# New priorities and engine choices for the first two batches and the weights of an attention and maxout kernel

## The chip, the cores and the metric

The kernel runs on one core of a Trainium2 chip. The time is device time in microseconds (us) of one execution of the whole program, and its figure is the median of several runs. The core's engines are TensorE (PE, matrix products), VectorE (DVE), ScalarE (ACT), GpSimd (POOL) and SyncE (SP, which here only issues DMAs). Each engine works through its own queue of instructions in a fixed order and waits where an instruction's inputs or buffers are not ready.

## The reference

Two attentions are added, and the sum goes through a maxout layer with an output projection. All is fp32.

```python
# q, k, v: 8 batches, 8 heads, 576 positions, head dim 64
factor = 4
scale = 1.0 / np.sqrt(D)
q_d = q.reshape(B, H, Sd, factor, D).mean(axis=3)      # and k_d, v_d
out_d = sm_attn(q_d, k_d, v_d)                         # 144 x 144 softmax attention
out_up = np.repeat(out_d, factor, axis=2)
mask = np.abs(pos[:, None] - pos[None, :]) < factor    # a band of 7 positions
scores = np.where(mask, scale * np.matmul(q, k.transpose(0, 1, 3, 2)), -1000000000.0)
out_local = np.matmul(softmax(scores), v)              # written out in the original
x = (out_up + out_local).transpose(0, 2, 1, 3).reshape(B * S, H * D)   # 4608 x 512
h = np.maximum(np.maximum(x @ w1, x @ w2), x @ w3)     # 512 -> 768
return h @ w_out                                       # 768 -> 512
```

## The kernel before

**Precision.** A first- or second-layer product is made of three fp32r matmuls. Each operand is split into a high part (a cast, `xhi`, `whi`, `hh`, `wo`) and a low part (what the cast lost, `xlo`, `wlo`), and hi x hi, lo x hi and hi x lo are added up in PSUM.

**Blocks.** The work is done by batch: 8 blocks of 512 tokens, and a ninth that holds the 64 positions left over from all batches. A block's input has four tiles of 128 channels, each with an `xhi` and an `xlo`. `mlp_in` makes the first layer: 6 column blocks, each with 3 accumulations of 12 matmuls (216 in all). `mlp_out` makes the second layer: 72 matmuls over 6 pieces of `w_out`. The matmuls of both go to PSUM tag `pm` (3 banks); attention's go mostly to `pa` (5 banks).

**Attention.** A head group `n` is four heads of a batch (`n` 0 and 1 are batch 0, 2 and 3 batch 1). Batches 0 and 1 are made by `dense`, step by step: `q` and `v` load, `qk` pools q and k (tiles `hp`, `qkT`), `s0` and `s1` make the banded scores of two heads each and their softmax (`mx`, `sm`, `z`), `tail` and `vd` pool v (`traw`, `vtail`, `hv`, `vd`), `sums` makes the pooled scores and their softmax (`nz`, `pd`, `rd`, `ptld`, and after a transpose `pt`, `ptt`), `pv` the pooled values (`od`), and `v0` and `v1` the banded values. `v0` and `v1` copy transposed weights out of PSUM (`y`), add `od` to the product, which gives a finished tile (`t` for batch 0, `x` for batch 1), and split it into `xhi` and `xlo`. The later batches take another way, with products on ACT and POOL, and are not touched by the change.

**Weights.** w1, w2 and w3 come as 64-bit words, in 6 blocks (`rawin`, 3072 words of 32 bits in each of 128 partitions), and w_out in 6 pieces (in `pvb`). `weight_split` (printed below) makes fp32 of them: an absolute value on ACT, a clamp, an `and`, two `or`s on DVE, the cast to the high part and the subtraction for the low part.

**What sets the order.** No engine order is written by hand. The functions record operations, each with a priority: the number that `at(...)` sets for the step, alone or per engine. `Recorder.place` then simulates the engines with a price for each operation: of the operations at an engine's head it takes the one that can start first, and of those that can start at the same time the one with the lowest priority number. An operation with several forms goes to the engine that would end it first. The order that comes out is emitted (line 495 issues every instruction, so that line stands in all rows) and is then fixed. So a priority says what goes first where two operations are ready together, and since every choice shifts what is ready next, a few numbers can reorder a whole stretch.

**The numbers.** `PLAN[0]` and `PLAN[1]` hold the steps of batches 0 and 1 with a priority for each; `WLOAD` has the priority of the six weight blocks' loads and `WMAKE` that of their splits, `WOUT` that of all that is done for w_out, `BEGIN` that of the first steps of head group 4. MLP work has -100, and the split of a finished tile -200. `HOMES` fixes copies and casts to ACT ("A"), to DVE ("D") or leaves them to the planner ("-"): `norm` (the normalising of `sm`, one letter for each pair of heads), `band` (the copies `y`), `hi` (the weight casts, six blocks and then six pieces), `xhi`, `od`, `pt` and `late` (the copies of `pt`'s last part and of `ptt`).

The core of the choice, from `place`:

```python
key = (t if t > now + PATIENCE[e] else now, o.prio, o.seq)
if pick is None or key < pick[0]:
    pick = (key, o, t)
```

Of the kernel before, what the change touches and what calls it, by code (L numbers as in the profile page):

```python
# [38 lines left out]
PLAN = (
    (  # L40
        ("q", 0, -2480.0),
        ("v", 0, 905.0),
        ("qk", 0, -2340.0),
        ("s0", 0, {"PE": 1990.0, "DVE": 540.0, "ACT": 1780.0}),
        ("s1", 0, {"PE": -1905.0, "DVE": 65.0, "ACT": 1135.0}),
        ("tail", 0, {"DVE": -405.0, "SP": 480.0}),
        ("q", 1, -975.0),
        ("v", 1, 1150.0),
        ("sums", 0, {"PE": -1675.0, "DVE": -1840.0, "ACT": 260.0}),
        ("vd", 0, {"DVE": -1715.0, "SP": 740.0}),  # L50
        ("qk", 1, -130.0),
        ("s0", 1, {"PE": 15.0, "DVE": -1045.0, "ACT": 1125.0}),
        ("s1", 1, {"PE": 1165.0, "DVE": 235.0, "ACT": 315.0}),
        ("tail", 1, {"DVE": 3360.0, "SP": 2255.0}),
        ("pv", 0, {"PE": -430.0, "ACT": 3475.0}),
        ("v0", 0, {"PE": 195.0, "DVE": -280.0, "ACT": 80.0}),
        ("v1", 0, {"PE": 1795.0, "DVE": 10.0, "ACT": -795.0}),
        ("sums", 1, {"PE": 1905.0, "DVE": 95.0, "ACT": -60.0}),
        ("vd", 1, 3095.0),
        ("pv", 1, {"PE": 95.0, "ACT": 6225.0}),  # L60
        ("v0", 1, {"PE": 1800.0, "DVE": -1230.0, "ACT": 3665.0}),
        ("v1", 1, {"PE": 1685.0, "DVE": 2800.0, "ACT": 1870.0}),
    ),
    (
        ("q", 0, 165.0),
        ("v", 0, -2485.0),
        ("qk", 0, 910.0),
        ("s0", 0, {"PE": 1930.0, "DVE": 60.0, "ACT": 230.0}),
        ("s1", 0, {"PE": 1090.0, "DVE": 1560.0, "ACT": 1425.0}),
# [1058 lines left out]
```

## Time and profile before

| | before |
|---|---|
| median of three runs | 720.01 us (719.7 to 720.5) |
| span of the profiled execution | 719.1 us |
| mean granted TensorE clock | 0.985 of full speed |
| PE busy | 687.1 us (96%), 4756 matmuls |
| DVE busy | 533.2 us (74%) |
| ACT busy | 400.8 us (56%) |
| POOL busy | 184.1 us (26%) |

The span runs from the first to the last instruction of one profiled execution; the runs' times have some 0.9 us around it. Busy shares are averages over the whole span. The kernel has two parts: a start of some 140 us, in which weights and the first batches are made ready, and a long rest in which the nine blocks of the MLP follow each other. The page's other parts are the slices of the span, the DMA queues, the chain of waits that ended last, and the costliest groups of instructions. `PEclk` is the granted TensorE clock: 1.00 is 2.4 GHz and 0.50 is 1.2 GHz.

### The profile page before, as it was taken

What the parts mean: (1) busy time and instruction counts of PE and PEld (TensorE: products, weight loads), DVE (VectorE), ACT (ScalarE), POOL (GpSimd) and SP (SyncE); (2) the same over time, 40 slices, a digit from 0 to 9 for tenths busy, and PEclk for the clock granted to TensorE, in tenths of its full rate; (3) what the DMA queues carried; (4) which work ended last, traced back from release to release, by engine and by line L of the source; (5) the groups of instructions that cost most, each with busy time, mean ns of one, the idle gap of its engine ahead of it and who ended that gap; (6) DMA issues with size and microseconds to landing.
All of it is one profiled execution on the core that took longest, in us unless ns stands there. A gap on an engine that the chain in (4) does not pass through costs nothing.

```text
span 719.1 us, 13533 instructions
## 1 busy us (share of the span) xinstructions
PE 687.1 (96%) x4756; PEld 555.2 (77%) x4756; DVE 533.2 (74%) x952; ACT 400.8 (56%) x1434; POOL 184.1 (26%) x250
## 2 busy tenths in 40 slices
PE   3679999999999999999999999999999999999996
PEld 2557777788878888888888888888888788888885
DVE  6989999887979688869887988796968687431220
ACT  4787774584738283928393739372948387221111
POOL 0000100062415061606150625060605156000000
PEclk9859999999999999999999999999999999999999
DMA  9952717465856677574848684758487673210002
GB/s 361 306 189 84 270 40 219 92 151 139 175 136 191 120 128 185 143 164 81 229 124 187 117 209 113 181 106 184 120 197 130 136 150 78 51 59 30 0 1 58
DMA packets 190817, 101.35 MB, mean 141 GB/s; under 512 B 161454, under 2 KB 166605, under 8 KB 189981
## 3 DMA queue, kind: packets, MB, share of 16 engines
q1 hardware_dynamic: 190749, 100.49, 56.4%
q8 instruction: 37, 0.61, 0.4%
q14 instruction: 31, 0.25, 0.1%
HBM read 71.23 MB, written 29.23 MB: 140 GB/s over the span
## 4 chain that ended last, share of the span: by engine, by line
PE 86%; DVE 7%; DMA 3%; ACT 2%; issue 1%; SPq 0%; ACTq 0%; DVEq 0%
PE pm L495 78%; PE pa L495 8%; DVE pvb L495 1%; DMA pvb<-in_wo_dram 1%; DMA wlo<-in_qk_dram 1%; DVE t L495 1%; DVE hh L495 1%; DVE nz L495 1%; DVE hp L495 1%; SPq L495 0%; DMA t<-xd 0%; DVE xlo_0r L495 0%; ACT pvb L495 0%; DVE mx L495 0%; ACT whi L495 0%
## 5 line engine op out<-in xcount | busy, mean ns | idle before, releaser
L495 PE MATMUL pm<-xhi_0r,whi_0r 128*128 128x512 f32 x648 | 253.9, 392 | 1.5 <-DVE t L495 1.5
L495 PE MATMUL pm<-xlo_0r,whi_0r 128*128 128x512 f32 x648 | 253.4, 391 | 0.0
L495 PE MATMUL pm<-xhi_0r,wlo_0r 128*128 128x512 f32 x648 | 253.3, 391 | 0.0
L495 POOL TENSOR_TENSOR pvb<-v,s 128x256 f32<-128x256 f32 x205 | 161.6, 820 | 203.7 <-DVE s L495 87.3
L495 ACT ACTIVATE pvb<-v,s 128x64 f32<-128x64 f32 x748 | 186.7, 342 | 7.8 <-DMA v<-in_v_dram 3.9
L495 PEld LDWEIGHTS pm<-xhi_0r,whi_0r 128*128 128x128 f32 x648 | 121.6, 188 | 27.7 <-DVE t L495 1.9
L495 PEld LDWEIGHTS pm<-xhi_0r,wlo_0r 128*128 128x128 f32 x648 | 121.7, 188 | 25.8 <-issue 0.6
L495 PEld LDWEIGHTS pm<-xlo_0r,whi_0r 128*128 128x128 f32 x648 | 121.7, 188 | 25.7 <-issue 0.8
L495 DVE TENSOR_TENSOR t<-pm,t 128x512 f32<-128x512 f32 x108 | 74.0, 685 | 81.7 <-PE pm L495 78.7
L495 DVE TENSOR_TENSOR pvb<-pvb 128x768 f32<-128x768 f32 x112 | 107.2, 957 | 5.5 <-POOL pvb L495 2.4
L495 ACT CAST hh_1r<-t 128x512 fp32r<-128x512 f32 x54 | 33.5, 621 | 101.7 <-DVE t L495 101.7
L495 PE MATMUL pm<-wo_0r,hh_1r 128*128 128x512 f32 x216 | 84.1, 392 | 1.4 <-ACT wo_0r L495 1.3
L495 PE MATMUL pm<-wo_1r,hh_1r 128*128 128x512 f32 x216 | 84.9, 393 | 0.0
L495 PE MATMUL pm<-wo_0r,hh_0r 128*128 128x512 f32 x216 | 84.4, 391 | 0.0
L495 ACT ACTIVATE pd<-pa,nz 128x144 f32<-128x144 f32 x90 | 33.2, 382 | 29.3 <-issue 12.6
L495 PEld LDWEIGHTS pm<-wo_0r,hh_1r 128*128 128x128 f32 x216 | 40.5, 188 | 10.9 <-ACT wo_0r L495 1.8
L495 ACT COPY t<-pm 128x512 f32<-128x512 f32 x54 | 31.6, 585 | 30.9 <-PE pm L495 30.9
L495 DVE TENSOR_TENSOR hh_0r<-t,hh_1r 128x512 fp32r<-128x512 f32 x54 | 39.2, 726 | 12.3 <-ACT hh_1r L495 12.2
L495 PEld LDWEIGHTS pm<-wo_1r,hh_1r 128*128 128x128 f32 x216 | 40.6, 188 | 9.8 <-issue 1.0
L495 PEld LDWEIGHTS pm<-wo_0r,hh_0r 128*128 128x128 f32 x216 | 40.6, 188 | 8.4
L495 ACT CAST xhi_0r<-t 128x512 fp32r<-128x512 f32 x30 | 18.7, 622 | 50.5 <-DVE t L495 47.3
L495 ACT COPY y<-pm 128x512 f32<-128x512 f32 (+1 forms) x43 | 23.8, 585 | 25.5 <-PE pm L495 24.8
(139 smaller groups left out, 678.8 us busy)
## 6 DMA issues: line engine op xcount, KB each, us to landing
v<-in_v_dram SPq DMA_DIRECT2D x55, 320.0 KB
qk<-in_qk_dram SPq DMA_DIRECT2D x30, 582.0 KB
out_dram<-y SPq DMA_DIRECT2D x36, 256.0 KB
scr<-sm SPq DMA_DIRECT2D x56, 140.0 KB
xd<-x SPq DMA_DIRECT2D x112, 64.0 KB
t<-xd SPq DMA_DIRECT2D x28, 256.0 KB
wo<-in_wi_dram SPq DMA_DIRECT2D x4, 1536.0 KB
pdd<-pd SPq DMA_DIRECT2D x48, 80.0 KB
```

The costliest lines, as they stand in the source:

```text
L495: getattr(self.engines[o.eng], method)(*map(real, args), **{k: real(x) for k, x in kw.items()})
```

## The change

Only numbers and letters in tables are replaced. The recorded operations, their shapes, the buffers and the planner stay as they are; the planner, given the new numbers, puts out another order, and some copies, casts and products are issued on another engine. `TAGS` (the PSUM banks of the steps) stays. Of the 44 priorities in `PLAN` nearly all are new; two lines of each batch stand for them.

```diff
-WLOAD = (450.0, 580.0, 2390.0, 260.0, -1745.0, 515.0)
+WLOAD = (450.0, -1828.0, 6751.0, -403.0, -6952.0, -281.0)
...
-WOUT = {"DVE": 60.0, "ACT": 2015.0, "SP": 1935.0}
+WOUT = {"DVE": 1421.0, "ACT": 2677.0, "SP": 8859.0}
...
-        ("sums", 0, {"PE": -1675.0, "DVE": -1840.0, "ACT": 260.0}),
-        ("vd", 0, {"DVE": -1715.0, "SP": 740.0}),
+        ("sums", 0, {"PE": -2104.0, "DVE": 10182.0, "ACT": -512.0}),
+        ("vd", 0, {"DVE": -12092.0, "SP": 531.0}),
...
-        ("sums", 0, {"PE": 820.0, "DVE": -605.0, "ACT": -1890.0}),
-        ("vd", 0, {"DVE": -1505.0, "SP": -115.0}),
+        ("sums", 0, {"PE": -3902.0, "DVE": -1542.0, "ACT": -12950.0}),
+        ("vd", 0, {"DVE": -8932.0, "SP": -7558.0}),
...
-HOMES = {"norm": "AA-A--A-", "band": "A-AADA-AAD-AA---", "hi": "-DAAAAADA-AA", "xhi": "--AA-AAA", "od": "AA--", "pt": "DAAA", "late": "--A-"}
+HOMES = {"norm": "AA--AAAA", "band": "AAA--A-A---AA-AD", "hi": "---AAA--AA-A", "xhi": "A----AA-", "od": "AAAD", "pt": "DAAA", "late": "-ADA"}
...
-BEGIN = {"PE": 775.0, "DVE": 1695.0, "ACT": 255.0, "POOL": 1095.0, "SP": 510.0}
+BEGIN = {"PE": 1249.0, "DVE": 3436.0, "ACT": -2804.0, "POOL": 5826.0, "SP": -6586.0}
```

The orders of the two kernels show what that does at three places. A row is an operation with output and inputs by the program's names and the output's shape.

DVE's queue at the end of batch 0. The last tile of batch 0 is the `t` that is read from `pm_147` (`t_441`) before and from `pm_145` (`t_447`) after; its low part is the `xlo_0r` that follows it. `sm_189`, `nz_143`, `rd` and `pd_175` are softmaxes of batch 1, `mx` maxima of banded scores, `wo_74` and `wo_75` blocks of raw weights.

Before:

```order
L495 TENSOR_TENSOR sm_189<-sm_189,z_188 128x560
L495 TENSOR_REDUCE mx_243<-pa_117 128x4
L495 TENSOR_SCALAR nz_143<-nz_143 128x6
L495 RECIPROCAL rd_193<-nz_143 128x6
L495 TENSOR_TENSOR ptld_89<-pd_175,rd_193 128x2x32
L495 TENSOR_TENSOR t_441<-pm_147,od_372 128x512
L495 TENSOR_TENSOR pd_175<-pd_175,rd_193 128x2x144
L495 TENSOR_TENSOR pd_175<-pd_175,rd_193 128x4x128
L495 TENSOR_TENSOR ptld_89<-pd_175,diag_104 128x2x32
L495 SCALAR_TENSOR_TENSOR wo_74<-wo_74 128x1536
L495 TENSOR_TENSOR traw_115<-traw_115 128x128
L495 TENSOR_TENSOR xlo_0r<-t_441,xhi_0r 128x512
```

After:

```order
L495 TENSOR_REDUCE mx_184<-pa_233 128x4
L495 TENSOR_SCALAR pvb_99<-pvb_99 128x1536
L495 TENSOR_REDUCE mx_243<-pa_305 128x4
L495 TENSOR_TENSOR vd_449<-hv_282 128x256
L495 TENSOR_TENSOR xlo_0r<-t_608,xhi_0r 128x512
L495 TENSOR_REDUCE mx_243<-pa_117 128x4
L495 TENSOR_TENSOR t_447<-pm_145,od_373 128x512
L495 TENSOR_TENSOR traw_112<-traw_112 128x64
L495 SCALAR_TENSOR_TENSOR wo_75<-wo_75 128x1536
L495 TENSOR_REDUCE nz_143<-pa_119 128x3
L495 TENSOR_TENSOR xlo_0r<-t_447,xhi_0r 128x512
```

The last row is DVE's 118th before and its 94th after: `xlo` of the last tile stands 24 rows earlier, and the `sm`, `rd` and `pd` products of batch 1 that stood ahead of it now stand behind it or on ACT.

ACT's queue ahead of the copy `pt` of head group 2 (batch 1's first). Before, the rows from the last `mx` of the stretch on; after, from the end of the pooled exponentials on.

Before:

```order
L495 ACTIVATE mx_243<-mx_243 128x8
L495 ACTIVATE sm_251,z_250<-pa_307,mx_243 128x70 x3
L495 CAST xhi_0r<-t_441 128x512
L495 ACTIVATE sm_251,z_250<-pa_307,mx_243 128x70
L495 ACTIVATE sm_251,z_250<-pa_117,mx_243 128x70 x4
L495 CAST whi_0r<-wo_74 128x1536
L495 COPY pt_257<-pa_231 128x4x128
```

After:

```order
L495 ACTIVATE pd_175,nz_143<-pa_119,nz_143 128x144
L495 ACTIVATE pd_175,nz_143<-pa_238,nz_143 128x144
L495 ACTIVATE sm_195<-sm_195,z_194 128x70 x8
L495 COPY t_608<-pm_208 128x512
L495 CAST hh_0r<-t_516 128x512
L495 ACTIVATE sm_251<-sm_251,z_250 128x70 x8
L495 COPY pt_284<-pa_233 128x4x128
```

Sixteen normalising products of `sm` (two rows of eight) and MLP copies and casts now stand on ACT ahead of `pt`.

SP's queue where the pieces of w_out are loaded (`pvb_99<-in_wo_dram`, six in all), among transfers of v, q and k, and of banded scores (`scr`).

Before:

```order
L495 DMA pvb_99<-in_wo_dram 128x1024
L495 DMA v_165<-in_v_dram 128x640
L495 DMA v_138<-in_v_dram 128x640
L495 DMA pvb_99<-in_wo_dram 128x1024
L495 DMA qk_91<-in_qk_dram 128x1164
L495 DMA qk_95<-in_qk_dram 128x1164
L495 DMA scr_1280<-sm_189 64x8x70 x2
L495 DMA scr_1280<-sm_251 64x8x70 x2
L495 DMA pvb_99<-in_wo_dram 128x1024 x2
L495 DMA s_1363<-scr_1280 128x16x7
```

After:

```order
L495 DMA pvb_99<-in_wo_dram 128x1024
L495 DMA v_138<-in_vw_dram 70x512
L495 DMA v_141<-in_v_dram 128x640
L495 DMA pvb_99<-in_wo_dram 128x1024 x2
L495 DMA v_165<-in_v_dram 128x640
L495 DMA v_138<-in_v_dram 128x640
L495 DMA qk_91<-in_qk_dram 128x1164
L495 DMA qk_95<-in_qk_dram 128x1164
L495 DMA scr_1394<-sm_195 64x8x70 x2
L495 DMA scr_1394<-sm_251 64x8x70 x2
```

The last two pieces, behind two `qk` and four `scr` transfers before, stand ahead of them after.

## Rows read from the trace of the kernel before

**Rows 1.** Page, part 1: busy time, share of the span and instructions

```profile
PE 687.1 (96%) x4756; PEld 555.2 (77%) x4756; DVE 533.2 (74%) x952; ACT 400.8 (56%) x1434; POOL 184.1 (26%) x250
```

**Rows 2.** Busy time of each engine by stretch of the whole span

```profile
core 0: us, PE busy (x) PEld busy (x) DVE busy (x) ACT busy (x) POOL busy (x), PEclk, DMA share, GB/s
0.00:43.02 43.02, 20.62 (x257) 14.86 (x258) 35.89 (x74) 27.97 (x124) 1.20 (x5) 0.86 0.98 335
43.02:64.32 21.30, 19.59 (x247) 15.43 (x248) 18.82 (x41) 14.95 (x58) 0.46 (x1) 0.79 0.35 110
64.32:136.80 72.48, 71.14 (x613) 56.03 (x613) 68.36 (x112) 45.52 (x130) 3.72 (x7) 1.00 0.52 151
136.80:712.80 576.00, 575.78 (x3640) 468.89 (x3640) 410.12 (x729) 311.75 (x1124) 178.70 (x237) 1.00 0.56 127
712.80:719.10 6.30, 0.00 (x0) 0.00 (x0) 0.00 (x0) 0.59 (x1) 0.00 (x0) 0.87 0.29 83
```

**Rows 3.** PE in order of time: start, us, instruction [idle before, releaser]

```profile
62.22 0.39 PE L495 MATMUL pm<-xlo_0r,whi_0r 128*128 128x512 f32 x1
62.45 0.39 PE L495 MATMUL pm<-xhi_0r,wlo_0r 128*128 128x512 f32 x1
64.32 0.50 PE L495 MATMUL pm<-xhi_0r,whi_0r 128*128 128x512 f32 x1 [1.48 <-DVE t L495]
...
136.80 0.96 PE L495 MATMUL pm<-wo_0r,hh_1r 128*128 128x512 f32 x3 [1.34 <-ACT wo_0r L495]
```

**Rows 4.** DVE in order of time

```profile
48.78 0.68 DVE L495 COPY y<-pm 70x512 f32<-70x512 f32 x1
49.38 0.41 DVE L495 CAST xhi_0r<-t 128x512 fp32r<-128x512 f32 x1
...
63.58 0.68 DVE L495 TENSOR_TENSOR t<-pm,od 128x512 f32<-128x512 f32 x1
...
67.16 0.69 DVE L495 TENSOR_TENSOR xlo_0r<-t,xhi_0r 128x512 fp32r<-128x512 f32 x1
```

**Rows 5.** DVE, 0 to 140 us, groups by form: count | busy, mean ns

```profile
L495 DVE TENSOR_TENSOR hp<-qk 128x576 f32<-128x576 f32 x10 | 7.5, 753 | 3.7 <-DMA qk<-in_qk_dram 3.7
...
L495 DVE TENSOR_TENSOR qkT<-hp 128x288 f32<-128x288 f32 x10 | 4.6, 458 | 0.6
...
L495 DVE TENSOR_TENSOR pd<-pd,rd 128x512 f32<-128x512 f32 x3 | 2.1, 686 | 0.0
...
L495 DVE TENSOR_TENSOR vd<-hv 128x256 f32<-128x256 f32 x4 | 1.6, 412 | 0.0
...
L495 DVE TENSOR_TENSOR sm<-sm,z 128x560 f32<-128x560 f32 x2 | 1.5, 734 | 0.0
...
L495 DVE CAST whi_0r<-hh 128x1536 fp32r<-128x1536 f32 x1 | 1.0, 960 | 0.0
```

**Rows 6.** Busy time of each engine, the second part of the half clock

```profile
43.00:51.80 8.80, 8.78 (x71) 6.95 (x75) 7.14 (x14) 7.35 (x18) 0.46 (x1) 0.50 0.34 96
```

**Rows 7.** SP's issues and ACT in order of time, at pieces of w_out

```profile
110.38 0.33 SPq L495 DMA_DIRECT2D pvb<-in_wo_dram  x1
...
122.26 2.41 SPq L495 DMA_DIRECT2D pvb<-in_wo_dram  x1
...
114.64 0.69 ACT L495 ACTIVATE pvb<-pvb 128x512 f32<-128x512 f32 x1 [1.08 <-DMA pvb<-in_wo_dram]
...
131.15 0.67 ACT L495 ACTIVATE pvb<-pvb 128x512 f32<-128x512 f32 x1 [1.82 <-DMA pvb<-in_wo_dram]
```

**Rows 8.** ACT, 0 to 140 us, groups by form

```profile
L495 ACT ACTIVATE sm<-sm,z 128x70 f32<-128x70 f32 x32 | 8.2, 357 | 0.2 <-DVE z L495 0.2
...
L495 ACT ACTIVATE pvb<-wo 128x1536 f32<-128x1536 f32 x4 | 6.5, 1618 | 0.0
```

**Rows 9.** POOL in order of time

```profile
35.02 1.00 POOL L495 TENSOR_TENSOR traw<-traw 128x128 f32<-128x128 f32 x1 [34.58 <-DMA traw<-in_vt_dram]
...
48.19 0.46 POOL L495 TENSOR_TENSOR traw<-traw 128x128 f32<-128x128 f32 x1 [12.17 <-DMA traw<-in_vt_dram]
```

More of the change, by code (lines that the diff above doesn't have):

```diff
@@ L39 @@
+WOUT = {"DVE": 1421.0, "ACT": 2677.0, "SP": 8859.0}
 PLAN = (
     (
[L41 to L48, printed above, removed]
-        ("sums", 0, {"PE": -1675.0, "DVE": -1840.0, "ACT": 260.0}),
-        ("vd", 0, {"DVE": -1715.0, "SP": 740.0}),
@@ L51 @@
[L51 to L60, printed above, removed]
@@ new lines @@
+        ("q", 0, -7008.0),
+        ("v", 0, 928.0),
+        ("qk", 0, 1557.0),
+        ("s0", 0, {"PE": 4001.0, "DVE": 165.0, "ACT": 1165.0}),
+        ("s1", 0, {"PE": -6408.0, "DVE": -2547.0, "ACT": -3897.0}),
+        ("tail", 0, {"DVE": -7971.0, "SP": 414.0}),
+        ("q", 1, -394.0),
+        ("v", 1, 1053.0),
+        ("sums", 0, {"PE": -2104.0, "DVE": 10182.0, "ACT": -512.0}),
+        ("vd", 0, {"DVE": -12092.0, "SP": 531.0}),
+        ("qk", 1, 6717.0),
+        ("s0", 1, {"PE": 1524.0, "DVE": 825.0, "ACT": 1515.0}),
@@ new lines @@
+        ("s1", 1, {"PE": -6575.0, "DVE": -1051.0, "ACT": 13711.0}),
+        ("tail", 1, {"DVE": 2199.0, "SP": 1517.0}),
+        ("pv", 0, {"PE": 4444.0, "ACT": 17291.0}),
+        ("v0", 0, {"PE": 4255.0, "DVE": -1186.0, "ACT": -5694.0}),
+        ("v1", 0, {"PE": 2488.0, "DVE": -6929.0, "ACT": 4049.0}),
+        ("sums", 1, {"PE": 13041.0, "DVE": -1149.0, "ACT": 2803.0}),
+        ("vd", 1, 3277.0),
+        ("pv", 1, {"PE": -7891.0, "ACT": 7139.0}),
+        ("v0", 1, {"PE": 3844.0, "DVE": -7455.0, "ACT": 9443.0}),
@@ new lines @@
+        ("v1", 1, {"PE": -1446.0, "DVE": 2591.0, "ACT": -2121.0}),
+    ),
+    (
+        ("q", 0, 85.0),
+        ("v", 0, -1487.0),
+        ("qk", 0, -425.0),
+        ("s0", 0, {"PE": -198.0, "DVE": -898.0, "ACT": -2616.0}),
+        ("s1", 0, {"PE": 1997.0, "DVE": 72.0, "ACT": 8363.0}),
+        ("tail", 0, {"DVE": 3522.0, "SP": 1499.0}),
+        ("sums", 0, {"PE": -3902.0, "DVE": -1542.0, "ACT": -12950.0}),
+        ("vd", 0, {"DVE": -8932.0, "SP": -7558.0}),
+        ("pv", 0, {"PE": 1764.0, "ACT": 9231.0}),
+        ("v0", 0, {"PE": -6771.0, "DVE": 1122.0, "ACT": -734.0}),
+        ("v1", 0, {"PE": 17.0, "DVE": -2126.0, "ACT": -3854.0}),
+        ("q", 1, 1410.0),
+        ("v", 1, 0.0),
+        ("qk", 1, 2143.0),
+        ("s0", 1, {"PE": -14795.0, "DVE": -5189.0, "ACT": 9511.0}),
+        ("s1", 1, {"PE": -2345.0, "DVE": 6201.0, "ACT": 838.0}),
+        ("tail", 1, {"DVE": 5460.0, "SP": -3433.0}),
+        ("sums", 1, {"PE": -1703.0, "DVE": 47.0, "ACT": 14406.0}),
+        ("vd", 1, {"DVE": 4100.0, "SP": -1766.0}),
+        ("pv", 1, {"PE": 866.0, "ACT": 2815.0}),
+        ("v0", 1, {"PE": -9397.0, "DVE": -5288.0, "ACT": -1936.0, "SP": 8356.0}),
+        ("v1", 1, {"PE": 216.0, "DVE": -7183.0, "ACT": 382.0, "SP": 750.0}),
```

23 lines of the change are left out of this document (1 added, 22 removed).

## The prediction

> **What bounds the kernel now.** I read the page first: TensorE (PE) is busy for 96% of the span [rows 1]. An engine that is full cannot be helped by a new order, so the next view was PE's busy time by stretch [rows 2]. The reader is to see there where PE is not full. From 136.80 us to its last matmul at 712.80 it is busy for 575.78 of 576.00 us. From 64.32 to 136.80 it lacks 1.34 us, from 43.02 to 64.32 it lacks 1.71 us, and in the first 43.02 us it lacks 22.4 us. The last 6.3 us are the copy and store of the last output. The matmuls themselves are the same in both kernels, so the time can move by three things alone: PE's gaps before 136.80, work at half clock, and new gaps.
>
> Who is late in these stretches? VectorE (DVE) is busy for 18.82 of 21.30 us and 68.36 of 72.48 us there [rows 2], so it is near its limit wherever PE still has a gap. PE in order of time [rows 3] shows the two gaps that count: 1.48 us before 64.32, ended by DVE's add `t`, and 1.34 us before 136.80, ended by ScalarE's (ACT) cast of a piece of w_out. DVE in order of time [rows 4] tells why the first is there: `t` is the fourth and last tile of batch 0, the add that makes it starts at 63.58 and its low part `xlo` at 67.16, because DVE's queue holds other work ahead of it. After 64.32 PE has batch 1 to fill in, and it does not stop again until 136.80. So the start lasts as long as DVE needs for what stands ahead of batch 0's last tile.
>
> **The change part by part.** The new numbers change no operation; they change the queues.
>
> *DVE ahead of batch 0's last tile.* In the old order the fourth `xlo` is row 118 of DVE's queue, in the new one row 94: 24 fewer instructions are ahead of it. Counting by kind, these go behind it or to another engine: two `hp` and two `qkT` sums of batch 1, one `sm` normalising, two `vd` sums, the six small instructions and the two large `pd` products of batch 1's pooled softmax, one `nz` maximum, two casts `xhi` and one copy `y` (now ACT's), and some small ones; one whole weight cast `whi` comes to DVE. By mean durations [rows 5] the large ones are 2 x 0.753 + 2 x 0.458 + 0.734 + 2 x 0.412 + 0.686 = 4.7 us, less 0.960 for the cast; the second `pd` product and the small ones, 17 more in all at about 0.3 us each, bring the sum to 8.9 us. The starts of neighbours lie 0.08 us closer than the durations (0.68 us lasting, 0.60 from start to start [rows 4]), and 24 x 0.08 = 1.9, so DVE's queue is shorter by 8.9 - 1.9 = 7.0 us at this place. With DVE's waits unchanged `xlo` starts at 67.16 - 7.0 = 60.2 and ends at 60.8.
>
> *What PE makes of it.* PE does not gain 7.0 us, since in the old order it ran 24 matmuls of the first layer (three accumulations over tiles 0 to 2) before it stopped. In the new queue the same 24 are interleaved with the fourth tile: the 21st reads its `xlo`. Matmuls follow each other by 0.23 us [rows 3], so the 24th ends at 60.8 + 4 x 0.23 = 61.7, where the old kernel stood at 64.32 with the same work done (both scores and the pooled scores of the third head group included). Gain: 2.6 us. PE's own work is the other limit. From 43.02 PE had no gap but these [rows 2], 8.78 us of it at half clock [rows 6]; in the new queue tile 1's product stands 3.4 us earlier for DVE (by the same count, row 75 against row 82), and PE, without gaps and with the clock returning at 51.8 as before, comes to the same 61 to 62. So the two limits lie together, and I take 2.6.
>
> *ACT.* It takes over the normalising of batch 1's first head group: 16 small products at 8.2/32 = 0.26 us [rows 8], 4.1 us, where DVE needed two instructions of 0.73. They stand ahead of ACT's copy `pt`, for which PE waits in front of batch 1's pooled values. PE comes there 26 matmuls later in its queue than before (62 first-layer matmuls against 36), 5.9 us, less the 2.6 won. Cover is thus 3.3 us plus ACT's own idle time against 4.1 us and some copies. The bounds are 0 (ACT's idle time takes it up; it is busy for 45.52 of 72.48 us [rows 2]) and the whole 4.1; I take 0.4, near the lower end, because the queue up to the copy holds waits of ACT for DVE which the shorter DVE queue shortens too.
>
> *w_out.* The last piece's `lo` is row 222 of DVE's queue before and row 212 now; by the same count 5.6 us less work is ahead of it. PE wants piece 4 after 18 matmuls of the second layer instead of 24, and after `pa` work that stood earlier: some 130.5 on the new clock. By DVE's queue the piece is there by then, if its load is. In the old kernel the loads of pieces 4 and 5 were the last of a row of q, k and score transfers: issued from 122.26 on, the first was waited for until 131.15 [rows 7]. In the new SP queue they stand ahead of these. I take the 1.34 us as won; the bounds are 1.34 won and all of the 2.6 given back.
>
> *Loads, first 40 us.* The SP queue differs in four places there, by one transfer each, and I cost that at nothing: DVE and ACT read their first weights from 15 us on in both.
>
> *POOL.* Two `vd` sums go from DVE to POOL. The same 128x128 sum on POOL took 0.46 us beside a waiting DVE and 1.00 us beside a busy one [rows 9]; on DVE a `vd` is 0.41 [rows 5]. That counts as 0.8 us off DVE above. The Trainium skill speaks against it: "SBUF — State Buffer", section "SBUF: two separate sides", says that GpSimd and a VectorE instruction with two SBUF inputs lock a shared port pair, and the one that comes second is blocked for the whole instruction. The doubled row agrees with it for POOL's side; by that rule DVE would lose about what it gives away, and the 7.0 us would be 5.5 to 6.2.
>
> *The sum.* -2.6 - 1.3 + 0.4 = -3.5 us. The profiled span is 719.1 us and the median of the runs 720.0, so 0.9 us lie around the span; 719.1 - 3.5 + 0.9 = 716.5.
>
> **The rivals.**
>
> *Given back at w_out.* PE arrives 2.6 us earlier at second-layer pieces whose loads are as crowded as before (8.9 us from issue to use against 4.3 for the piece issued at 110.38 [rows 7]). For: the cast of piece 4 stands behind ACT's first touch of piece 5 in both queues, so one late load holds both. Against: the loads come earlier in SP's queue. PE would then wait until 134 to 136 again: 718.3 to 720.0, at the middle 719.2.
>
> *DVE's waits go too.* The 7.0 us assume DVE's old waits between 43.02 and 64.32, 2.5 us [rows 2]. If PE hands over its scores sooner, they vanish, `xlo` ends at 58.3 and PE gains up to 5.1: -5.1 - 1.3 = -6.4, 713.6. Against: PE's work at half clock [rows 6] has no room for it unless the clock returns before 51.8, where the old kernel had 8.8 us of unbroken matmuls first.
>
> *ACT becomes the bound: slower.* Place: `pt` and the two copies `y` of batch 1's first head group, each behind ACT work that was not there or stood later: the 4.1 us of normalising, and a 1.62 us absolute value of a weight block [rows 8]. If ACT has no idle time to take them up, PE waits 4.1 + 1.6 = 5.7 us between 70 and 80 us: -3.9 + 5.7 = +1.8, 721.8. It decides from 3.9 us of such waits on. For: every copy that PE waits for in the old first 43 us is ACT's. Against: ACT is idle for over a third of the stretch.
>
> *Little comes of it.* The queues move, but the half clock lasts longer and eats the lead: each further us at half clock costs half a us, so 7 us more of it give 720.0.
>
> **How the numbers follow.** Forecast 716.5 (own range 715.0 to 718.2): 0.50. Given back at w_out: 0.20, of which 0.08 still under 718.6. DVE's waits go too: 0.16. ACT as the bound: 0.11. Little comes of it: 0.03. A measurement of this kernel can tell about 0.2% (1.4 us) from no change. Faster by more: 0.50 + 0.08 + 0.16 = 0.74; within: 0.12 + 0.03 = 0.15; slower: 0.11. The range runs from 713.2, which leaves out the lower part of the second rival, to 720.0, which leaves out the slower one.
>
> **What the profile of the changed kernel would show.** PE's wait for `t` near 64 gone, its first gap-free stretch beginning near 61 to 62; the fourth `xlo` on DVE ending near 61; DVE in 15 to 64 us as full as before; PE's wait for ACT's `wo` cast under 0.5 us near 130; PE ending at about 709. Wrong would make it: a PE wait for `pt`, `y` or `sm` of over 1 us between 65 and 130, a half clock beyond 54 us, or a gap of PE at a later batch, of which the old kernel has none and my sum assumes none.

## The result, and the profile after the change

The changed kernel takes 713.86 us (median of six runs, 713.41 to 716.26) against 720.25 us for the kernel before in the same comparison (six runs, 719.7 to 722.7). The ratio is 0.9912 with a 95% interval from 0.9892 to 0.9931, so 6.4 us are gained where 3.5 were forecast. In the profiled executions the span went from 719.1 to 711.7 us.

Part 1 of the page of the changed kernel, which answers to [rows 1]: busy time, share of the span, instructions.

```profile
PE 686.0 (96%) x4756; PEld 555.6 (78%) x4756; DVE 522.1 (73%) x934; ACT 401.2 (56%) x1433; POOL 193.7 (27%) x266
```

PE does the same work. DVE has 11.1 us less, POOL 9.6 us more, ACT much the same in all. The busy time by stretch (columns as in [rows 2]), cut at the same places of the program as there where these can be found again (59.68 is the start of the nineteenth first-layer matmul, which stood at 64.32 before; 705.36 is the end of PE's last matmul):

```profile
0.00:43.02 43.02, 25.89 (x303) 19.57 (x303) 36.08 (x74) 30.42 (x136) 2.37 (x7) 1.00 0.98 338
43.02:59.68 16.66, 14.89 (x205) 11.13 (x203) 16.03 (x23) 12.28 (x42) 2.79 (x2) 0.90 0.43 126
59.68:128.00 68.32, 68.32 (x588) 54.86 (x587) 67.22 (x123) 49.28 (x150) 6.43 (x7) 1.00 0.42 138
128.00:705.36 577.36, 576.94 (x3667) 470.01 (x3665) 402.75 (x717) 308.67 (x1106) 182.13 (x251) 1.00 0.55 129
```

Three things stand in it. In the first 43.02 us PE is busy for 25.89 us where it was 20.62: its gaps there shrank from 22.4 to 17.1 us. In the next stretch DVE idles for 16.66 - 16.03 = 0.63 us, where it idled for 2.48. From 59.68 on PE has no gap up to 128, so the wait before 136.80 [rows 3] is gone.

How much of the gain is made in the first stretch can be read off PE's queue, which holds the same matmuls in the same order there. First two rows of the kernel before, then the same two of the changed one; the brackets hold the idle time before and what ended it:

```profile
39.86 1.95 PE L495 MATMUL pm<-x_0r,sm 128*70 128x128 f32 x8 [4.36 <-ACT whi L495]
43.02 0.48 PE L495 MATMUL pm<-y,x 70*64 70x64 f32 x2 [1.20 <-ACT y L495]
```

```profile
36.95 1.92 PE L495 MATMUL pm<-x_0r,sm 128*70 128x128 f32 x8
38.98 0.45 PE L495 MATMUL pm<-y,x 70*64 70x64 f32 x2
```

So PE is 4.04 us ahead by then, more than half of the whole gain: the wait of 4.36 us for ScalarE's exponentials is gone (the banded scores of head group 1 lie in buffers named `whi` and `wlo`). These need the maxima `mx` of head group 1's second scores from DVE, which start at 31.58 us and no longer at 36.30.

PE and DVE of the changed kernel in order of time, at the places of [rows 3] and [rows 4]:

```profile
53.06 0.50 PE L495 MATMUL pm<-xhi_0r,whi_0r 128*128 128x512 f32 x1
...
59.68 0.39 PE L495 MATMUL pm<-xhi_0r,wlo_0r 128*128 128x512 f32 x1
```

```profile
58.72 0.68 DVE L495 TENSOR_TENSOR xlo_0r<-t,xhi_0r 128x512 fp32r<-128x512 f32 x1
```

The first first-layer matmul moved from 57.17 to 53.06 us, the nineteenth from 64.32 to 59.68, and it no longer waits for `t`. From 53.1 to 705 us PE's waits by releaser (total us, count, largest) are down to one:

```profile
PE pm L495 <- ACT y L495: 0.3, 1, 0.3
```

The span's 7.4 us divide into 4.64 by the nineteenth matmul, 1.34 by the wait for the cast of w_out, and 1.4 that stands in no single wait. Counted by the n-th first-layer matmul, the lead is 8.4 us at the 601st (255.32 against 263.69) and still at the 1501st (551.88 against 560.32), and 7.4 from the 1621st on (599.12 against 606.53). So 2.4 us more are won behind the start, and 1.0 is given back between 552 and 599 us, where the changed kernel has two waits that the old one lacks, 0.12 us at 563.04 and 0.30 at 577.21.

### The profile page after: what moved, and what is told of

It is laid out like the page before. It is cut to its first block, busy times and chain, and to the rows that moved or that the text cites. A ratio compares the mean times of both kernels' runs of the same rounds, so it can differ in the third digit from the quotient of the medians.

```text
span 711.7 us, 13513 instructions
## 1 busy us (share of the span) xinstructions
PE 686.0 (96%) x4756; PEld 555.6 (78%) x4756; DVE 522.1 (73%) x934; ACT 401.2 (56%) x1433; POOL 193.7 (27%) x266
## 5 line engine op out<-in xcount | busy, mean ns | idle before, releaser
L495 POOL TENSOR_TENSOR pvb<-v,s 128x256 f32<-128x256 f32 x212 | 158.0, 778 | 205.5 <-DVE s L495 139.7
L495 ACT ACTIVATE pvb<-v,s 128x64 f32<-128x64 f32 x720 | 179.8, 340 | 17.1 <-DVE s L495 9.4
L495 ACT CAST hh_0r<-t 128x512 fp32r<-128x512 f32 x54 | 33.5, 619 | 102.3 <-DVE t L495 102.3
L495 PE MATMUL pm<-wo_1r,hh_0r 128*128 128x512 f32 x216 | 84.7, 392 | 0.0
L495 PEld LDWEIGHTS pm<-wo_0r,hh_1r 128*128 128x128 f32 x216 | 40.5, 188 | 8.8 <-issue 0.4
L495 PEld LDWEIGHTS pm<-wo_1r,hh_0r 128*128 128x128 f32 x216 | 40.5, 188 | 8.8 <-issue 0.6
L495 DVE TENSOR_TENSOR hh_1r<-t,hh_0r 128x512 fp32r<-128x512 f32 x53 | 38.2, 721 | 11.2 <-ACT hh_0r L495 11.1
```

What stands on the lines that cost most here:

```text
L495: getattr(self.engines[o.eng], method)(*map(real, args), **{k: real(x) for k, x in kw.items()})
```

## The experiments

Of the twelve kernels, two are the changed kernel as it is and three have other tables. Seven leave every number in the tables alone and alter the finished queues instead. A function put behind `place` moves instructions to another place in their own engine's queue, or issues one a second time; engines and all else stay. An entry of `MOVES` is (engine, first, last, ahead of), places in the engine's queue counted from 0; one of `TWICE` is (engine, place). A place is that of a recorded operation, and some operations are several instructions. No kernel leaves out any of the computation. The added function shifts the source line of all instructions to L541. Each kernel was compared with the kernel before on the same chip. The medians of before there were 722.30 us (beside b_early, b_late, b_both and b_sp), 721.33 (beside a_same, a_sp, a_twice and b_homes) and 722.65 (beside a_again, a_homes, a_twice1 and c_mix).

```diff
+        for e, first, last, ahead in MOVES:
+            ops = was[e][first : last + 1]
+            q = [o for o in queues[e] if o not in ops]
+            at = q.index(was[e][ahead])
+            queues[e] = q[:at] + ops + q[at:]
+        for e, k in TWICE:
+            o = was[e][k]
+            o.forms[e] = list(o.forms[e]) * 2
...
-        out = self.place()
+        out = self.edited(self.place())
```

### Moving a few of DVE's instructions in the kernel before

If the start lasts as DVE's queue does ahead of the last tile of batch 0, a shift of a few DVE instructions in the old queue might buy part of the gain. Two such shifts, and both together.

The first takes the two maxima `mx` of the second scores of head group 1 and two `nz` instructions ahead of the subtraction that makes the second weight block's `wlo`:

```diff
+MOVES = (('DVE', 46, 46, 44), ('DVE', 48, 48, 44), ('DVE', 50, 50, 44), ('DVE', 52, 52, 44))
```

> The kernel before with four instructions moved on DVE: the maxima of head group 1's second scores and the two small ones ahead of the pooled exponentials go ahead of one weight subtraction (1.75 us) and one normalising (0.73 us). Nothing else moves. Theory A (the start is a chain: DVE's maxima, ACT's exponentials, the bank that PE waits for 4.36 us at 39.86): that wait falls by 2.4 to 2.7 us, the first matmul of the first layer comes at 54.5 to 55 instead of 57.17; the last tile of batch 0, whose DVE queue is as long as before, comes earlier only by DVE's own waits there (2.3 us), so the time falls by 1.5 to 2.3 us, to about 718.3. Theory B (only the work that stands on DVE ahead of the last tile counts, as in the prediction): the wait at 39.86 falls, but the time stays within 0.5 us of 720.2.

Measured: 722.13 us, ratio 1.0009 [0.9987, 1.0030], no change. PE in order of time in this run, then DVE:

```profile
36.98 1.07 PE L541 MATMUL pm<-x_0r,sm 128*70 128x128 f32 x4 [1.63 <-ACT whi L541]
...
40.55 0.85 PE L541 MATMUL pm<-x_0r,sm 128*70 128x128 f32 x3 [2.51 <-DVE t L541]
...
63.51 0.50 PE L541 MATMUL pm<-xhi_0r,whi_0r 128*128 128x512 f32 x1 [1.47 <-DVE t L541]
```

```profile
39.81 0.68 DVE L541 TENSOR_TENSOR t<-pm,od 128x512 f32<-128x512 f32 x1
```

The wait ahead of the banded values that the move aimed at fell from 4.36 to 1.63 us, but a new wait of 2.51 us for a `t` stands 3.6 us later. That `t` has not become late: it started at 40.02 us before. All the work that changed places stands ahead of it in either order, so it is as late as it was, and the longer wait had hidden it. In the changed kernel it starts at 38.20. The nineteenth matmul gained 0.8 us and waits for `t` as long as before.

The second takes seven operations (eight instructions) that stand ahead of batch 0's last `xlo`, seven of the instructions for batch 1 and one `or` of a weight block, and puts them behind it:

```diff
+MOVES = (('DVE', 86, 86, 110), ('DVE', 92, 92, 110), ('DVE', 98, 98, 110), ('DVE', 104, 107, 110))
```

> The kernel before with work of batch 1 (one hp and qkT sum, one vd sum, one sm normalising, the pd products, one or of a weight block: 5.3 us) moved on DVE behind the last tile of batch 0. Nothing else moves. Theory B: the add t of the last tile starts at about 61.2 instead of 63.58 and its xlo at about 62; PE's wait of 1.48 us before 64.32 goes, and by the prediction's count the whole gain is 2.6 us: 717.6. Theory A: the wait of 1.48 us is all that can go, since PE has 18 matmuls of the first layer until 62.84 and not more: 718.8. In both the last w_out piece may wait longer by what is won, which would take the gain back: then 720.

Measured: 725.52 us, ratio 1.0045 [1.0025, 1.0065], slower. PE in order of time, a window (columns as in [rows 2]), and DVE ahead of the last `t`:

```profile
63.77 0.50 PE L541 MATMUL pm<-xhi_0r,whi_0r 128*128 128x512 f32 x1 [0.68 <-DVE t L541]
...
68.26 0.88 PE L541 MATMUL pa<-x_0r,pd 128*128 128x128 f32 x6 [2.83 <-DVE pd L541]
```

```profile
69.60:73.00 3.40, 3.40 (x10) 2.67 (x9) 3.37 (x8) 2.62 (x5) 0.00 (x0) 0.52 0.09 15
```

```profile
62.45 0.17 DVE L541 TENSOR_SCALAR nz<-nz 128x6 f32<-128x6 f32 x1 [1.10 <-ACT pd L541]
```

The wait for `t` halves; it was expected to go. With the shorter queue DVE waits 1.10 us for ScalarE's exponentials `pd`, and `t` starts at 63.03 where 61.2 was expected. And PE has only 24 first-layer matmuls ahead of batch 1's pooled transposes in this order, so it runs into `pd`, which now comes late: 2.83 us. The clock row adds to it: after that gap PE was busy for 3.40 us at a granted clock of 0.52, nearly all of it at the 1.2 GHz level, some 1.6 us more.

Both moves together:

```diff
+MOVES = (('DVE', 46, 46, 44), ('DVE', 48, 48, 44), ('DVE', 50, 50, 44), ('DVE', 52, 52, 44), ('DVE', 86, 86, 110), ('DVE', 92, 92, 110), ('DVE', 98, 98, 110), ('DVE', 104, 107, 110))
```

> The kernel before with both moves. If the first gaps and the queue ahead of the last tile bound the start one behind the other, they add up to more than either: PE stands at its 19th matmul of the first layer at 60 to 60.5 (64.32 before, 59.68 in the changed kernel), and the time falls by 3.8 to 4.3 us if PE's later wait at w_out stays at 1.3, to 716.2. If w_out's pieces bound what follows, PE's wait there grows from 1.34 to 4 to 5 us and the time stays at 718.5 to 720.

Measured: 726.25 us, ratio 1.0054 [1.0033, 1.0074]. The nineteenth matmul starts at 62.48, 1.8 us earlier than before, and the `pd` wait of 2.84 us stands at 66.97. Neither expectation for the two together came true. What the three runs say holds for these two moves: in the first a second instruction stands as late as the one that was helped, in the second what was passed has a reader that PE needs within some microseconds. Whether other small moves would do is not shown. The changed kernel has another order and, beside it, less work on DVE (11.1 us over the whole span).

### The loads of w_out

In the kernel before, the load of piece 4 is put ahead of the score transfers in SP's queue:

```diff
+MOVES = (('SP', 65, 65, 61),)
```

> The kernel before with the load of w_out's piece 4 moved on SP ahead of the four score transfers that are issued from 118.70 on. By the prediction (the row in SP's queue is what makes the piece late) PE's wait of 1.34 us at 136.80 goes: 718.9. If the buffer is what holds it (piece 4 takes the half of pvb that piece 2 gives back when its low part is done at 121.1), the load starts 1.2 us earlier at most, the wait falls by 1.0 us at most: 719.2; and if the score transfers that now stand behind it are as urgent, nothing is won: 720.2.

Measured: 720.79 us, ratio 0.9988 [0.9968, 1.0008]. The load is issued 1.40 us earlier than in [rows 7], and from 64 to 713 us PE's waits hold no `wo` any more:

```profile
120.86 0.33 SPq L541 DMA_DIRECT2D pvb<-in_wo_dram  x1
```

```profile
PE pm L541 <- DVE t L541: 1.5, 1, 1.5
PE pm L541 <- DVE hh_0r L541: 0.4, 1, 0.4
PE pm L541 <- ACT y L541: 0.3, 1, 0.3
```

Two small waits at 211 and 216 us take back part of the 1.34 us. The median is 1.5 us lower, about the term of the sum, but the interval reaches 1, so the time alone does not show it. The opposite edit in the changed kernel puts the load of the last piece behind the v and qk loads again:

```diff
+MOVES = (('SP', 58, 58, 63),)
```

> The changed kernel with the load of w_out's last piece moved on SP behind two v and two q/k loads, about where it stood before; nothing else moves. In the trace of the changed kernel that load is issued at 119.03, the q/k loads at 125.6 to 126.4. ACT's absolute value of the last piece stands ahead of its cast of piece 4 (125.65 to 126.31), for which PE comes at about 127. If the rows of SP are what the w_out gain hangs on, as in the prediction, ACT gets the last piece at about 131, PE waits 4 to 6 us before the second layer's piece 4, and 4 to 6 us of the gain are lost. If the pieces are held by their buffers and not by SP's rows, nothing changes (under 0.5 us).

Measured: 728.02 us, ratio to before 1.0081 [1.0055, 1.0108], where the changed kernel itself stands at 0.9924 on this chip. SP's issue, then ACT and PE in order of time, and the window around:

```profile
130.31 0.38 SPq L541 DMA_DIRECT2D pvb<-in_wo_dram  x1
```

```profile
137.60 0.66 ACT L541 ACTIVATE pvb<-pvb 128x512 f32<-128x512 f32 x1 [11.57 <-DMA pvb<-in_wo_dram]
...
140.07 0.79 PE L541 MATMUL pm<-wo_0r,hh_0r 128*128 128x512 f32 x1 [9.15 <-ACT wo_0r L541]
```

```profile
135.90:146.10 10.20, 6.03 (x34) 4.41 (x34) 5.11 (x10) 3.37 (x7) 0.00 (x0) 0.50 0.32 64
```

One transfer in the wrong place costs the whole lead and more, twice the 4 to 6 us expected: a PE wait of 9.15 us, and some 3 us for 6.03 us of PE's work at half clock around it. So in the changed kernel the place of this load is worth some 12 us by the medians (728.02 against 715.68), and of the 1.34 us that the forecast took from it none was given back. The traced execution is 3 us longer still, with another half clock at 53.9 to 60.8 us, ahead of its nineteenth matmul (62.88).

### The changed kernel beside itself

Twice the changed kernel as it is was run beside its variants, for a measure of how far its own times and traces spread.

```diff
 (nothing is edited)
```

> The changed kernel as it is, on this chip, for the runs beside it: 0.991 of the time before (0.989 to 0.993), PE's first first-layer matmul at 53, its 19th at 59.7, no wait of PE over 0.5 us behind it.

> The changed kernel once more, as the measure for the three beside it on this chip: 0.990 to 0.994 of the time before.

Measured: 715.68 us, ratio 0.9924 [0.9899, 0.9949], and 715.31 us, 0.9908 [0.9883, 0.9934]. The times agree, the traces less: the half clock sits elsewhere in each. In the trace of the result it is at 45.1 to 48.5 us (the first window below), in the first repetition at 53.1 to 59.9 (the second window and the first row of PE, of that run), in the second at 22.9 to 39.9 and 46.8 to 50.2 (the third window and the second row). The last row is of a_twice below, whose queues are those of the changed kernel up to 79 us; its half clock is at 30.2 to 40.5.

```profile
45.10:48.50 3.40, 3.40 (x31) 2.73 (x32) 3.37 (x5) 2.15 (x3) 2.07 (x1) 0.50 0.22 57
```

```profile
53.10:59.90 6.80, 6.80 (x62) 5.01 (x61) 5.20 (x9) 6.74 (x34) 0.00 (x0) 0.50 0.35 104
22.90:39.90 17.00, 12.39 (x127) 9.02 (x128) 16.83 (x35) 15.25 (x70) 2.60 (x3) 0.50 1.04 327
```

```profile
62.25 0.39 PE L495 MATMUL pm<-xhi_0r,wlo_0r 128*128 128x512 f32 x1
...
59.56 0.39 PE L495 MATMUL pm<-xhi_0r,wlo_0r 128*128 128x512 f32 x1
...
58.48 0.39 PE L541 MATMUL pm<-xhi_0r,wlo_0r 128*128 128x512 f32 x1
```

In the second repetition the nineteenth matmul starts at 59.56 in spite of 20.4 us of half clock, of which 17 us lie early on, where PE waits for DVE and ACT anyway (it is busy for 12.39 of 17.00 us). In the first, the half clock falls on the unbroken first-layer matmuls, and the nineteenth starts at 62.25. In a_twice it starts at 58.48. So the queues allow 58.5 us, not the 59.7 of the result, and a half clock at the wrong place adds up to 3.8 us in one execution. Nor is the gain the clock's: the kernel before has 20.5 us of half clock (31.3 to 51.8), the second repetition as much, and it is 4.8 us ahead at the nineteenth matmul.

### Is DVE the bound? One subtraction twice

Early in the changed kernel, the subtraction for the second block's `wlo` (near 44 us) is issued twice, which adds some 2 us to DVE's queue ahead of batch 0's last tile (the pair lasts 3.95 us, the single one 1.74):

```diff
+TWICE = (('DVE', 69),)
```

> The changed kernel with one DVE instruction issued twice ahead of batch 0's last two tiles: the subtraction that makes the low part of weight block 1 (1.74 us, at 44.3 us). By the prediction (the start lasts as long as DVE needs for what stands ahead of the last tile) everything behind it comes 1.7 us later and the time grows by 1.5 to 1.8 us. If the queue of DVE ahead of the last tile is by now shorter than what PE has to do until it needs that tile's bank (the add t ends at 56.4, PE needs the bank at 59.7: 3.2 us), the time grows by under 0.5 us.

Measured: 719.71 us, ratio 0.9956 [0.9935, 0.9978], against 0.9908 for the changed kernel on the same chip, so +4.4 us by the medians, where 1.5 to 1.8 or under 0.5 was expected. DVE and PE in order of time, then two windows:

```profile
44.27 3.95 DVE L541 TENSOR_TENSOR wlo_0r<-hh,whi_0r 128x1536 fp32r<-128x1536 f32 x2
...
49.21 0.48 PE L541 MATMUL pa<-ptt,vtail 64*64 64x144 f32 x8 [1.68 <-DVE vtail L541]
```

```profile
49.60:63.30 13.70, 13.17 (x150) 9.85 (x147) 10.25 (x16) 8.98 (x40) 1.87 (x1) 0.50 0.37 119
55.68:65.68 10.00, 10.00 (x74) 7.42 (x73) 7.93 (x14) 7.59 (x36) 0.00 (x0) 0.62 0.21 77
```

About 2 us of DVE work turn into a PE wait of 1.68 us that was not there, and the first first-layer matmul starts at 55.68, 2.6 us later than in the result. From there to the nineteenth PE is busy throughout and needs 10.00 us instead of 6.62, because the half clock reaches to 63.3 here. The traced execution is the slowest of the twelve (721.97 us), so the clock's part is smaller in the median run. So DVE's queue at this place does set the start, with the clock on top. That the changed start has slack on DVE there is refuted.

Later, the fourth block's subtraction (near 79 us) is issued twice:

```diff
+TWICE = (('DVE', 122),)
```

> The changed kernel with one DVE instruction issued twice: the subtraction that makes the low part of weight block 3 (1.74 us, near 78 us), where PE has no gap. If DVE still carries the kernel up to w_out (it is busy for 97% of 64 to 120 us, and the cast of piece 4 ends 0.6 us before PE comes for it), the second one is lost but for that slack: PE waits 1 us more near 127, the time grows by 1.0 to 1.7 us. If PE alone bounds the kernel behind 60 us, it grows by under 0.3 us.

Measured: 715.08 us, ratio 0.9914 [0.9894, 0.9934], beside 0.9924 for the changed kernel on that chip: no cost. The pair on DVE, and the largest of PE's waits between 52 and 705 us:

```profile
79.39 3.54 DVE L541 TENSOR_TENSOR wlo_0r<-wo,whi_0r 128x1536 fp32r<-128x1536 f32 x2
```

```profile
PE pa L541 <- ACT pt L541: 0.4, 1, 0.4
```

DVE was busy for 67.22 of 68.32 us between 59.68 and 128, and I had taken that for a limit. It is not one: what DVE makes there is wanted later, so 1.7 us more of it shows in no wait above 0.4 us. A busy share of 98% and a bound are two things, and the same test that cost 4.4 us at 44 us cost nothing at 79.

### The engines alone, the priorities alone, a part of each

The kernel before with the new letters of `HOMES`, all priorities old:

```diff
-HOMES = {"norm": "AA-A--A-", "band": "A-AADA-AAD-AA---", "hi": "-DAAAAADA-AA", "xhi": "--AA-AAA", "od": "AA--", "pt": "DAAA", "late": "--A-"}
+HOMES = {"norm": "AA--AAAA", "band": "AAA--A-A---AA-AD", "hi": "---AAA--AA-A", "xhi": "A----AA-", "od": "AAAD", "pt": "DAAA", "late": "-ADA"}
```

> The kernel before with the new HOMES alone (the engines of the copies, casts and normalising); all priorities stay, and the planner makes its order again. In that order the first tiles of batch 0 and the first-layer matmuls come earlier by about what they do in the changed kernel (18 of them done 4 to 5 us earlier), but the transposes of batch 1's pooled softmax still stand behind the first 24 first-layer matmuls, and DVE makes that softmax no earlier. Theory (engines and order gain only together): PE waits some 3 us for pd there, and the time ends within 1.5 us of before. Rival (the relief of DVE by the new engines is the gain): 4 to 5 us faster.

Measured: 717.08 us, ratio 0.9944 [0.9924, 0.9964], so 4.2 us by the medians, three quarters of the 5.65 us that the changed kernel gains on this chip. PE in order of time, and the first window:

```profile
59.81 0.39 PE L495 MATMUL pm<-xhi_0r,wlo_0r 128*128 128x512 f32 x1
...
65.63 0.62 PE L495 MATMUL pa<-x_0r,pd 128*128 128x128 f32 x2 [1.58 <-ACT pd L495]
```

```profile
0.00:43.02 43.02, 23.22 (x270) 17.42 (x272) 36.28 (x70) 30.82 (x128) 0.93 (x5) 0.86 0.94 332
```

The nineteenth matmul is at 59.81, as in the changed kernel, at a granted clock of 0.86 in the first 43 us, and there is no wait for w_out. What is missing to the changed kernel is a wait of 1.58 us for `pd`: in this order only 36 first-layer matmuls stand ahead of the transposes that read it, in the changed kernel 50. My theory, that the letters alone are worth at most 1.5 us, fell. The planner makes its order anew for the new letters, so this run does not part the engines from the order that follows from them. What it does show is a shorter DVE queue: 98 rows and 51.73 us of DVE's work stand ahead of batch 0's last `xlo`, where 117 rows and 57.55 us stood before. The Trainium skill, "Perfetto Trace Analysis", section "Optimizing Scalar/DVE Operations", says that offloading work to ScalarE may make sense where DVE is saturated; this run agrees with it at -4.2 us.

The changed kernel with the old letters, all priorities new:

```diff
-HOMES = {"norm": "AA--AAAA", "band": "AAA--A-A---AA-AD", "hi": "---AAA--AA-A", "xhi": "A----AA-", "od": "AAAD", "pt": "DAAA", "late": "-ADA"}
+HOMES = {"norm": "AA-A--A-", "band": "A-AADA-AAD-AA---", "hi": "-DAAAAADA-AA", "xhi": "--AA-AAA", "od": "AA--", "pt": "DAAA", "late": "--A-"}
```

> The changed kernel with the old HOMES; all new priorities stay, and the planner makes its order again. The old HOMES alone were taken away from the other side (the kernel before with the new HOMES: 0.994 of before). If the engines are the gain and the priorities add a little, this one stands near before, 0.998 to 1.002. If the priorities only fit the new engines, it is worse than before: in its order the 19th first-layer matmul stands some 14 us later than in the changed kernel, behind a wait of several us for the copies y and the pooled scores; 8 to 12 us slower than the changed kernel: 1.003 to 1.009 of before.

Measured: 732.54 us, ratio 1.0155 [1.0125, 1.0186]. The largest of PE's waits between 31 and 725 us:

```profile
PE pm L495 <- DVE y L495: 8.0, 1, 8.0
```

It was expected to be slower than before, but by 0.3 to 0.9%. Without the new engines the new priorities put batch 0 behind work that DVE cannot finish in time: PE waits 8.0 us for a copy `y`. The nineteenth matmul starts at 81.3. The two halves of the change do not add up: -4.2 us, +9.9 us, and together -7.3, each by the medians on its own chip.

Last, a mixture that might have beaten both: the new priorities for batch 1 and for the weights' loads and splits, with the new letters `norm`, `band`, `xhi` and `od`, and all else old.

```diff
-WLOAD = (450.0, 580.0, 2390.0, 260.0, -1745.0, 515.0)
+WLOAD = (450.0, -1828.0, 6751.0, -403.0, -6952.0, -281.0)
...
-        ("sums", 0, {"PE": 820.0, "DVE": -605.0, "ACT": -1890.0}),
+        ("sums", 0, {"PE": -3902.0, "DVE": -1542.0, "ACT": -12950.0}),
...
-HOMES = {"norm": "AA-A--A-", "band": "A-AADA-AAD-AA---", "hi": "-DAAAAADA-AA", "xhi": "--AA-AAA", "od": "AA--", "pt": "DAAA", "late": "--A-"}
+HOMES = {"norm": "AA--AAAA", "band": "AAA--A-A---AA-AD", "hi": "-DAAAAADA-AA", "xhi": "A----AA-", "od": "AAAD", "pt": "DAAA", "late": "--A-"}
```

> A mixture of the two kernels: PLAN of batch 1, WLOAD, WMAKE and the letters norm, band, xhi and od of HOMES from the changed kernel; PLAN of batch 0, WOUT, BEGIN and the letters hi and late from before. In its order batch 0's first tiles come later than in the changed kernel (more DVE work ahead of the first), but the last tile earlier (1.2 us less DVE work ahead of its xlo), and no wait for w_out is to be seen in the order. If what counts is when PE has a full queue of first-layer matmuls, it is 0 to 1.5 us faster than the changed kernel; if the early gaps (32 to 37 us) cost their length and the half clock follows them, it is 1 to 3 us slower.

Measured: 723.50 us, ratio 1.0025 [1.0000, 1.0050], 8.2 us above the changed kernel on the same chip, which neither expectation had. The nineteenth matmul is at 59.98, so the start is as good as in the changed kernel, and yet nothing is gained. PE in order of time, later:

```profile
210.40 0.71 PE L495 MATMUL pa<-pt,vd 128*64 128x144 f32 x8 [1.24 <-DMA pt<-pdd]
...
219.22 0.73 PE L495 MATMUL pm<-xhi_0r,whi_0r 128*128 128x512 f32 x2 [1.51 <-ACT xhi_0r L495]
...
220.82 0.50 PE L495 MATMUL pm<-xlo_0r,whi_0r 128*128 128x512 f32 x1 [0.64 <-DVE xlo_0r L495]
```

PE waits 3.39 us in these three rows, with another half clock from 221.5 to 224.9, and 0.5 and 1.4 us more at 295 and 579 us. PE's last matmul ends at 714.6, behind the 712.80 of [rows 2]. My reading is that a lead at 60 us makes PE come earlier to every later batch, and that it waits where the queues behind are not early too; no run parts this from the other differences of the mixture's order. A good start is not enough. No version that beats the changed kernel was found.

## Why the prediction was right, and where its sizes were off

The sign and the main cause, a shorter DVE queue, held; the place held in part, since more than half of the gain is won before the stretch in which the sum looked for it. The time came out at 713.86, inside the range of 713.2 to 720.0 but 1.1 us below the forecast's own range of 715.0 to 718.2, and next to the rival "DVE's waits go too" (713.6). That the range holds it is owed to this rival, which had a chance of 0.16; the sum itself gave 3.5 of 6.4 us. DVE's waits, the matmuls counted for PE and ACT's term all made it too small.

**DVE ahead of batch 0's last tile: right, with the rival's condition.** The count of 7.0 us less in DVE's queue gave 60.2 for the start of the fourth `xlo` with DVE's waits unchanged; with the waits gone it would be 57.7. It started at 58.72. DVE's busy time up to there, before and after (columns as in [rows 2]):

```profile
0.00:67.16 67.16, 43.05 (x521) 32.77 (x522) 57.55 (x118) 45.12 (x192) 1.66 (x6) 0.85 0.74 249
```

```profile
0.00:58.72 58.72, 39.82 (x500) 29.95 (x501) 51.15 (x94) 41.74 (x177) 5.16 (x9) 0.97 0.84 283
```

DVE's work ahead of it is 6.4 us less, and its idle time 2.0 us less (7.57 instead of 9.61), together the 8.44 us by which the tile is earlier. So the count was good to 0.6 us, and the waits went with it. The reason given against that, that PE's work at half clock leaves no room, was wrong twice. PE was 4.04 us ahead in its queue at 38.98 us. And the half clock is no fixed cost of this stage: the nineteenth matmul stood at 59.8 and 59.6 in two other runs with long half clocks early on.

**The first 43 us: where the lead is won.** The prediction named 22.4 us of PE's gaps there and gave them no term in the sum; it priced the loads alone, at nothing. The stretch came in only beside the sum, as PE's own limit: tile 1's product 3.4 us earlier on DVE and PE without gaps, which was to come to the same 61 to 62. In the traced execution this limit is the one that holds: from 53.06 on nothing stops PE. Tile 1's `t` starts 4.5 us earlier (43.68 against 48.17), and 4.04 of the 4.64 us at the nineteenth matmul are won by 38.98. The new order does it: DVE makes the maxima that ScalarE and then PE wait for 4.7 us earlier, and the first `t` 1.8 us earlier. The run with the maxima moved alone (b_early) shows that they do not do it by themselves.

**What PE makes of it: the step that was mis-sized.** The prediction set the gain at 2.6 us because the old kernel had run 24 first-layer matmuls before it stopped, so that the 24th of the new order was compared with 64.32. The trace of before has 18 there, between 57.15 and 64.2 us (count | busy us, mean ns | idle):

```profile
L495 PE MATMUL pm<-xhi_0r,wlo_0r 128*128 128x512 f32 x6 | 2.5, 409 | 0.0
L495 PE MATMUL pm<-xlo_0r,whi_0r 128*128 128x512 f32 x6 | 2.4, 392 | 0.0
L495 PE MATMUL pm<-xhi_0r,whi_0r 128*128 128x512 f32 x6 | 2.3, 409 | 0.0
```

The nineteenth, at 64.32, opens the third accumulation (nine matmuls each over three tiles). The row names the add `t` as what ended its wait [rows 3], and the accumulation reads nothing that `t` makes: the program has three `pm` banks, two are in use, and `t` reads the third. So it waited for a PSUM bank, not for the tile's `xlo`. Six matmuls at 0.23 us are 1.4 us: the same working with the right count gives 4.0, and 4.64 was measured. I read the wait as one for data, where it was one for a buffer, and so counted six matmuls of the third accumulation as done that were not. In the changed kernel nothing waits there at all; the gain is 4.11 us of an earlier first matmul, plus the 1.48 us wait, less 0.97 us of scores that now stand among the first-layer matmuls.

**ACT: 0.4 us too dear.** No PE wait for `pt` is left in the changed kernel, so the normalising products that ACT took over are hidden. The rival "ACT becomes the bound" did not show in any of its places.

**w_out: right.** The wait of 1.34 us is gone, and no wait came in its place near 128. The run with the load late again shows the mechanism to be the place in SP's queue, by 12 us, far more than the 2.6 that the rival "Given back at w_out" could lose: that rival took its price from the old kernel's lateness, not from what one passed transfer can cost.

**POOL: the rule's price was about right.** Two sums of the changed kernel that POOL makes, each with what DVE did beside it:

```profile
36.72 1.01 POOL L495 TENSOR_TENSOR vd<-hv 128x256 f32<-128x256 f32 x1 [13.42 <-DVE hv L495]
...
37.06 1.21 DVE L495 TENSOR_TENSOR wlo<-wlo,rd 128x512 f32<-128x512 f32 x1
```

```profile
46.34 2.07 POOL L495 TENSOR_TENSOR hv<-v 128x256 f32<-128x256 f32 x1 [6.48 <-DMA v<-in_v_dram]
...
46.89 2.35 DVE L495 TENSOR_SCALAR pvb<-pvb 128x1536 f32<-128x1536 f32 x2
```

The product at 37.06 takes 1.21 us, where it took 0.68 at 43.00 us in the kernel before. The two instructions at 46.89 should take 1.8 us (one alone at 53.24 takes 0.95) and take 2.35. With 0.13 us at a third place (39.60) DVE loses 1.2 us; POOL's sum at 46.34 takes 2.07 us, and a similar one at 22.57 took 0.72. The Trainium skill, "SBUF — State Buffer", section "SBUF: two separate sides", has the two engines block each other at a shared port pair, and these rows agree with it. The 0.8 to 1.5 us that the prediction had by that rule, and left out of its sum, fit these 1.2 us. They are part of the measured 51.15, and by that rule the 7.0 us were to be 5.5 to 6.2, where 6.4 was measured.

**The rest.** 1.4 us of the span's gain lie behind the nineteenth matmul in no wait that the trace shows, and their cause stays open. The medians differ by 6.4 us where the two profiled executions differ by 7.4. In every run whose span is known the time is 1.8 us longer than the span (713.52 and 711.7 here), not the 0.9 that the prediction put around it by setting one execution's span beside the median of others. So the profiled execution of before was some 0.7 us above its median and that of the changed kernel 0.3 below, which is that 1.0 us. The forecast of 716.5 does not change by it, since it is the median of before less 3.5.

## What to carry to other kernels

Before counting what a full engine gains from a shorter queue elsewhere, settle whether the wait that ended last was for data or for a buffer, because that says how much of the following work was already done. Test a busy engine by issuing one of its instructions twice at two places: 98% busy cost nothing at one place, and 2 us of work cost 4.4 us at the other. A stretch with 22 us of gaps is worth a term of its own in the sum, even where no bound stands out in it. The new engine choices, with the order that the planner made for them, carried three quarters of this gain; the new priorities paid only together with them, and one load left late cost more than the whole lead.
